# Two block rows of the causal attention turned by VectorE and a copy through DRAM, not by TensorE

## The chip, the cores and the metric

One core of one Trainium2 chip runs the whole program. The metric is device time in microseconds from launch to the end, taken as the median of three runs. A profiled execution gives the trace that the sections below read; its span runs from the first to the last instruction on the core.

## The reference

Two layers of attention follow each other. The first is a sliding window with four sink positions; the second is a mixture of four causal attentions, of which each position takes the two that its gate ranks highest.

```python
# layer 1: q, k, v are (4, 8, 768, 64); n_sink = 4, window = 128
scores = q @ k.T / 8
keep   = (pos_k < 4) | ((0 <= pos_q - pos_k) & (pos_q - pos_k < 128))
x      = softmax(where(keep, scores, -1e9)) @ v        # heads side by side: (4, 768, 512)

# layer 2: 4 experts, head size 64
w = softmax over the two largest of x @ w_gate
for e in range(4):
    qe, ke, ve = x @ wq[e], x @ wk[e], x @ wv[e]
    a    = softmax(where(causal, qe @ ke.T / 8, -1e9))  # (768, 768), lower triangle
    out += w[e] * (a @ ve @ wo[e])
```

## The kernel before

A sequence of 768 positions is six blocks of 128. Work comes in units. A unit of the first layer, `(b, n, 0)`, is a batch entry and a pair of heads; a unit of the second, `(b, n, 1)`, is a batch entry and a pair of experts (n is 0 or 1), so there are 16 of the one and 8 of the other. All is in fp32, products of the second layer in three passes over high and low parts.

`wide_rows` does the second layer's attention. A block row i has i + 1 key blocks, so rows 4 and 5 have five and six. Each row goes through the same steps, for both experts e: TensorE makes the scores in PSUM tiles `b` (L825, in two parts for five or six blocks, by `SPLIT`); VectorE masks, scales and takes the minimum of the negated scores into an SBUF tile `p` (L981); ScalarE takes the exponential with its sum (L989); `factor` makes one over the sum times the gate weight; GpSimd multiplies the row by it, in place (L996, `norm`). The row now has queries on the partitions, but the product with the values needs keys there. So `transposed` turns it part by part: TensorE transposes each 128x128 block in two halves of 64 partitions against `ident` (L878), into two PSUM tiles, which ScalarE (L707) or VectorE (L709) copies to `pt`, and then TensorE multiplies `pt` with the values into a PSUM tile `acc` (L851, called AV below). `finisher` splits `acc` into the high and low parts of `y` for the last product, `store`.

The first layer's `band_rows` uses the same steps on a band of two blocks, and the same transposes. Its q and k come from DRAM; for batch entries 1 to 3 they are loaded with their 32x32 squares already in swapped places (L1145), and VectorE transposes inside the squares (L799, L803).

The order of all instructions is made by `Plan` when the program is built: steps have a priority, costs and dependencies, and `emit` picks step after step for the five engines. `NUDGE` adds a number to the priority of single steps; `HURRY`, `STAY` and `BULK` weigh waiting, changes between kinds of matmul, and bulk. Where its plan has TensorE waiting, it puts matmuls on zeros (`fill`, L525). Buffers are rings (`kinds`: nine `p`, three `pt`, two `acc`). Each engine then runs its list strictly in order, and so does SyncE (SP), which issues every DMA.

TensorE runs four kinds of matmul, by how the array is split: transposes, scores and sink products (two row halves), AV (two column halves), and whole-array products (projections, values, `store`, called full below).

Of the kernel before, what the change touches and what calls it, by code (L numbers as in the profile page):

```python
# [37 lines left out]
    "busy_PE": 5.2, " ": -68.2, " busy_PE": 82.2, " busy_PE 0": 78.2, "sink_values_DVE": 13.5, " sink_values_DVE": -16.5,  # L38
    "load_SP": -45.6, " load_SP": 39.9, "again_SP": 20.9, " again_SP": 56.7, "sink_values_ACT": -27.6,
    " sink_values_ACT": 7.3, "sink_values_POOL": 52.1, " sink_values_POOL": 35.8, "sink_values_SP": -45.0,  # L40
    " sink_values_SP": -24.6, "weight_ACT": -52.5, " weight_ACT": 53.4, "weight_POOL": -34.8, " weight_POOL": 46.3,
    "000 ": -73.5, "000 load_SP": -144.1, "tr_PE": -1.9, "000 tr_PE": -132.5, "000 tr_PE 0": -105.3, "fn_DVEACT": -11.6,
    "000 fn_DVEACT": 132.8, "000 tr_PE 1": -54.6, "go_POOL": 0.7, "000 go_POOL": -36.7, "000 tr_PE 2": -47.6,
    "000 tr_PE 3": -19.2, "spread_POOL": -14.3, "000 spread_POOL": -25.7, "differences_POOL": 6.4,
    "000 differences_POOL": 24.4, "band_scores_PE": 0.5, "000 band_scores_PE": -115.3, "000 band_scores_PE 0": 8.1,
    "low_DVE": -53.0, "000 low_DVE": -79.5, "exp_ACT": 45.8, "000 exp_ACT": 63.9, "go_DVE": -42.9, "000 go_DVE": -204.0,
    "norm_POOL": -27.0, "000 norm_POOL": -84.7, "000 tr_PE 4": 23.5, "av_PE": -0.2, "000 av_PE": -0.9, "000 av_PE 0": -50.3,
    "000 band_scores_PE 1": -19.2, "000 tr_PE 5": -41.0, "000 av_PE 1": -26.4, "000 band_scores_PE 2": -53.5,
    "pick_DVE": -45.8, "000 pick_DVE": -22.7, "000 band_scores_PE 3": -19.7, "keep_POOL": -10.3, "000 keep_POOL": 6.5,
    "000 tr_PE 6": 35.3, "tri_DVE": -62.4, "000 tri_DVE": 59.9, "of_sinks_PE": -0.3, "000 of_sinks_PE": -1.5,  # L50
# [241 lines left out]
}  # L292

HURRY = 30.10
STAY = 41.79
BULK = -8.35
FILL_COST, FILL_KEEP, FILL_END = 220.0, 0.0, 130000.0
# [177 lines left out]
def kernel(  # L475
# [71 lines left out]
    def pool_cost(n):  # L547
        return 150 + 1.68 * n
# [18 lines left out]
    if banded:  # L567
# [28 lines left out]
        for t in (*slots["psk"], *slots["vs"]):  # L596
            nc.vector.memset(t.bitcast(F32), 0.0)
# [759 lines left out]
```

## Time and profile before

| | us |
|---|---|
| median of three runs (394.5 to 394.53) | 394.53 |
| the profiled execution, its own time | 394.46 |
| its span | 392.8 |
| TensorE busy | 383.0 |
| VectorE busy | 309.9 |
| ScalarE busy | 271.5 |
| GpSimd busy | 260.7 |

The 1.7 us between the profiled time and its span lie outside the recorded instructions. Busy time is a share of the span; idle time of an engine off the longest chain costs nothing. The granted clock of TensorE is full (1.0, its upper level) throughout.

### The profile page before, as it was taken

The numbers are of one execution on the slowest core, as the hardware profiler recorded it, in microseconds if no ns is written. First come the engines' busy times: TensorE is split into PE (matmuls) and PEld (weight loads), VectorE is DVE, ScalarE is ACT, GpSimd is POOL, SyncE is SP. The second block draws the span as 40 slices with busy tenths as digits, with TensorE's granted clock in tenths as the row PEclk, the third lists the DMA queues.
The fourth block names the chain that finished last, engine by engine and source line by source line (L and its number), as shares of the span: only waits on it lengthen the run. The fifth ranks groups of instructions, "written<-read, shape, count | busy, mean of one in ns | idle before, by whom it ended". The sixth has DMA issues, their size and how long they took to land.

```text
span 392.8 us, 12874 instructions
## 1 busy us (share of the span) xinstructions
PE 383.0 (98%) x4508; PEld 325.0 (83%) x4508; DVE 309.9 (79%) x1425; ACT 271.5 (69%) x970; POOL 260.7 (66%) x461
## 2 busy tenths in 40 slices
PE   6999999999999999999999999999999999999995
PEld 6777777988878888988888888988888888987874
DVE  5899999687999969679889959678679806748943
ACT  2898996256999957568869958549678804716830
POOL 5569999237999982668959864479958730038840
PEclk9999999999999999999999999999999999999999
DMA  7979997331165151523506200223000000012003
GB/s 164 220 148 172 197 174 127 56 49 43 43 100 105 44 107 55 83 83 82 82 2 119 47 0 5 40 109 95 2 3 2 3 3 2 2 53 109 3 28 134
DMA packets 124032, 28.42 MB, mean 72 GB/s; under 512 B 120576, under 2 KB 120576, under 8 KB 123968
## 3 DMA queue, kind: packets, MB, share of 16 engines
q1 hardware_dynamic: 123968, 27.61, 33.4%
q8 instruction: 35, 0.57, 0.6%
q14 instruction: 29, 0.24, 0.2%
HBM read 21.05 MB, written 6.29 MB: 70 GB/s over the span
## 4 chain that ended last, share of the span: by engine, by line
PE 81%; DVE 10%; POOL 3%; issue 2%; ACT 2%; DMA 1%; POOLq 0%; DVEq 0%; ACTq 0%
PE acc L851 18%; PE b L1177 18%; PE b L825 13%; PE b L878 10%; PE b L1204 9%; PE b L1251 9%; PE b L820 3%; DVE b L1078 2%; DVE p L1081 1%; PE acc L855 1%; DVE p L981 1%; DMA qn<-in_q_dram 1%; POOL v L680 1%; POOL p L1059 1%; DVE pt L709 1%
## 5 line engine op out<-in xcount | busy, mean ns | idle before, releaser
L996 POOL TENSOR_TENSOR p<-p,st 128x128 f32<-128x128 f32 (+5 forms) x96 | 87.2, 934 | 1.3
L707 ACT ACTIVATE pt<-b 128x256 f32<-128x256 f32 (+3 forms) x175 | 63.3, 396 | 12.6 <-PE b L878 8.8
L989 ACT ACTIVATE p<-p,st 128x384 f32<-128x384 f32 (+5 forms) x96 | 63.6, 669 | 9.4 <-DVE st L981 9.0
L825 PE MATMUL b<-ks,qs 64*128 64x260 f32 (+4 forms) x672 | 69.6, 323 | 0.4 <-DVE st L1081 0.2
L825 PEld LDWEIGHTS b<-ks,qs 64*128 64x128 f32 x672 | 53.0, 187 | 4.8 <-ACT pt L707 0.8
L878 PE MATMUL b<-ident,p 64*128 64x64 f32 x1120 | 55.2, 228 | 0.2 <-POOL p L1059 0.2
L878 PEld LDWEIGHTS b<-ident,p 64*128 64x128 f32 x1120 | 44.3, 138 | 11.8 <-issue 6.0
L1085 ACT ACTIVATE p<-p,st 128x132 f32<-128x132 f32 x128 | 51.1, 407 | 3.9 <-DVE st L1081 3.6
L981 DVE CUSTOM_DVE_ANT_0 p<-b,cmask 128x384 f32<-128x384 f32 (+3 forms) x96 | 45.3, 506 | 1.4 <-ACT o L707 1.1
L851 PE MATMUL acc<-pt,v 128*64 128x128 f32 x672 | 45.5, 278 | 0.6 <-DVE pt L709 0.5
L851 PEld LDWEIGHTS acc<-pt,v 128*64 128x64 f32 x672 | 36.2, 137 | 7.1 <-issue 3.9
L851 PE MATMUL acc<-pt,vn 128*64 128x128 f32 x448 | 41.5, 283 | 0.3 <-ACT p L989 0.3
L709 DVE COPY pt<-b 128x256 f32<-128x256 f32 (+3 forms) x81 | 34.6, 446 | 8.3 <-PE b L878 7.9
L1059 POOL TENSOR_TENSOR p<-p,st 128x520 f32<-128x520 f32 (+1 forms) x32 | 26.4, 834 | 14.8 <-DVE st L867 11.3
L1204 PE MATMUL b<-wvh,x 128*128 128x260 f32 x192 | 35.9, 285 | 0.0
L1177 PE MATMUL b<-x,wqh 128*128 128x256 f32 (+1 forms) x128 | 33.2, 345 | 0.1
L1104 POOL TENSOR_TENSOR p<-p,st 128x512 f32<-128x512 f32 x32 | 33.1, 1040 | 0.0
L1177 PE MATMUL b<-x,wkh 128*128 128x512 f32 (+1 forms) x128 | 32.8, 341 | 0.0
L1251 PE MATMUL b<-woh,y 128*128 128x512 f32 x96 | 32.8, 402 | 0.0
L1081 DVE CUSTOM_DVE_ANT_0 p<-b,pair_mask 128x132 f32<-128x132 f32 x128 | 32.6, 289 | 0.0
L1078 DVE COPY_PREDICATED b<-earlier,b 128x128 f32<-128x128 int32 x128 | 31.4, 288 | 1.2 <-PE b L820 1.1
L1052 ACT ACTIVATE p<-p,st 128x260 f32<-128x260 f32 (+1 forms) x64 | 29.0, 459 | 3.5 <-DVE st L1047 3.4
(132 smaller groups left out, 916.4 us busy)
## 6 DMA issues: line engine op xcount, KB each, us to landing
vn<-in_v_dram SPq DMA_DIRECT2D x32, 192.0 KB, 3.1
out_dram<-o SPq DMA_DIRECT2D x24, 256.0 KB, 2.0
qn<-in_q_dram SPq DMA_DIRECT2D x52, 96.0 KB, 2.4
kn<-in_k_dram SPq DMA_DIRECT2D x52, 96.0 KB, 2.4
qn<-in_q_dram SPq DMA_DIRECT2D x6, 192.0 KB, 4.1
kn<-in_k_dram SPq DMA_DIRECT2D x6, 192.0 KB, 4.4
o<-in_moe_wo_dram SPq DMA_DIRECT2D x2, 256.0 KB, 3.4
v<-in_moe_wk_dram SPq DMA_DIRECT2D x4, 128.0 KB, 3.8
```

Source lines behind the costliest of these rows:

```text
L707: nc.scalar.activation(dst(), src(), AF.Copy)
L825: nc.tensor.matmul(o, self.qs.t[hs, a, qs], self.ks.t[hs, b, ks], start=n == 0, stop=n == 2)
L851: nc.tensor.matmul(o[e * 64:e * 64 + 64], lhs, rhs, start=e not in self.begun, stop=last and self.done == len(self.steps))
L878: nc.tensor.transpose(t[g].t[:, n, :], x[gs], ident[gs, gs])
L981: nc.vector.tensor_tensor_reduce(out=one(e)[:, cs], in0=s2[e].t[:, :(c1 - c0) * 128], in1=mask(c0, c1), scale=times, scalar=st.t[:, 3, es] ...
L989: nc.scalar.activation(x, x, AF.Exp, bias=st.t[:, 0, es], scale=-1.0, accum_out=st.t[:, 1, es])
L996: nc.gpsimd.tensor_mul(x, x, st.t[:, 2, e:e + 1].to_broadcast([128, n * 128]))
L1078: nc.vector.copy_predicated(s2[e].t[:, :128], earlier.bitcast(I32), s2[e].t[:, SW:RW])
L1085: nc.scalar.activation(p.t[:, n, :], p.t[:, n, :], AF.Exp, bias=st.t[:, 0, n:n + 1], scale=-1.0, accum_out=st.t[:, 1, n:n + 1])
L1177: nc.tensor.matmul(t.t, w[a][:, c, es], X[b, c].t[:, x, cs], start=c == 0 and m == 0, stop=c == NCH - 1 and m == 2)
L1204: nc.tensor.matmul(t.t[:, :VW], X[b, c].t[:, a, qs], W["wv"][w][:, c, :], start=c == 0 and n == 0, stop=c == NCH - 1 and n == 2)
L1251: nc.tensor.matmul(t.t, Y[b, c].t[:, a, qs], W["wo"][w][:, c, :], start=c == 0 and n == 0, stop=c == EP - 1 and n == 2)
```

## The change

In five of the eight units of the second layer, rows 4 and 5 (five and six blocks) no longer go through `transposed`. A new function, `by_way_of_dram`, makes `norm` write the row into a second `p` tile with its 32x32 squares regrouped, lets VectorE transpose inside the squares, writes that tile to DRAM (`there`) with one DMA, and reads it back with four, one per 32 partitions, so that the squares change places. AV then takes its moving operand straight from that tile. In these units the two row groups are also done in reverse, rows 4 and 5 first. The set-up of the constant `lanes` moves ahead of the masks, that of `gsel`, `psk` and `vs` behind them. Nearly all of the 1200 entries of `NUDGE`, and three weights, have other numbers.

```diff
-HURRY = 30.10
-STAY = 41.79
-BULK = -8.35
+HURRY = 29.29
+STAY = 30.56
+BULK = -8.87
...
-        free = {PE: 2000.0, DVE: 3700.0, ACT: 2000.0, POOL: 6000.0, SP: 650.0}
+        free = {PE: 2000.0, DVE: 4500.0, ACT: 4000.0, POOL: 5300.0, SP: 650.0}
...
+    def by_way_of_dram(prio, acc, i, one, ps, cols, r, st, value):
 
-        for i in range(NB):
+        n, got, us = len(cols), [], []
+        for e in range(2):
+            u, there = buf("p", n * 128), buf("there", n * 128)
+            us.append(u)
+
+            def norm(u=u, e=e):
+                nc.gpsimd.tensor_mul(u.t.rearrange("p (b j c) -> p j b c", b=4, c=32), one(e).rearrange("p (j b c) -> p j b c", b=4, c=32),
+                                     st.t[:, 2, e:e + 1, None, None].to_broadcast([128, n, 4, 32]))
+
+            def back(u=u, there=there):
+                for b in range(4):
+                    nc.sync.dma_start(u.t[32 * b:32 * b + 32].rearrange("r (a x) -> r a x", a=4),
+                                      there.t.rearrange("(a r) (b x) -> b r a x", a=4, b=4)[b])
+            s = plan.step(prio - WIDE_N, {POOL: pool_cost(128 * n)}, norm, [r], [u], [ps[e], st])
+            s = plan.step(prio - WIDE_N, {DVE: 83 + 1.04 * 128 * n}, lambda u=u: nc.vector.transpose(u.t, u.t), [s], (), [u])
+            s = plan.step(prio - WIDE_N, {SP: 475}, lambda u=u, there=there: nc.sync.dma_start(there.t, u.t), [s], [there], [u], moves=MOVE * n)
+            got.append(plan.step(prio - WIDE_N - 10, {SP: 1900}, back, [s], (), [there, u], moves=MOVE * n))
+
+        def av():
+            acc.done += 1
+            for c, j in enumerate(cols):
+                for e in range(2):
+                    acc.add(i, e, value[0](j, e), us[e].t.rearrange("p (a j c) -> p j a c", a=4, c=32)[:, c], c == n - 1)
+        new, used = acc.bufs()
+        acc.steps.append(plan.step(prio + AV_LAG + 10, {PE: 218 * n}, av, got + value[1](cols), new, us + value[2] + used, fifo="av", mode="cols"))
+
+    def wide_rows(prio_of, pair, blocks, masks, value, weights, finish, groups, times=-scale, away=()):
+
+        for place, i in enumerate([i for lo, hi in (groups[::-1] if away else groups) for i in range(lo, hi)]):
...
             r = factor(prio - WIDE_N, st, sums, weights and (lambda i=i: weights[0](i)), weights and weights[1][i])
+            if i in away:
+                by_way_of_dram(prio, acc, i, one, ps, cols, r, st, value)
+                if i == hi - 1:
+                    finish(prio, acc)
+                continue
...
+    AWAY, MOVE = {u: (4, 5) for u in ((0, 0), (0, 1), (1, 0), (1, 1), (2, 0))}, 300
```

The first place is on TensorE, in the unit `(0, 0, 1)`. Before, the five-block row (tiles `p_91` and `p_92`, one for each expert) is turned by 20 transposes, of which the last six stand here; scores of the first layer and an AV on a turned part follow.

```order
L878 MATMUL b_120<-ident,p_92 128x64
L878 MATMUL b_123<-ident,p_92 128x64
L878 MATMUL b_120<-ident,p_91 128x64
L878 MATMUL b_123<-ident,p_91 128x64
L878 MATMUL b_120<-ident,p_92 128x64
L878 MATMUL b_123<-ident,p_92 128x64
L820 MATMUL b_121<-kx_82,qn_64 128x260
L820 MATMUL b_122<-kx_82,qn_64 128x260
L851 MATMUL acc_125<-pt_98,v_0_83 64x128 x4
```

After, no transpose of that row is left. Its tiles (now `p_91` and `p_93`) go into AV as they came back from DRAM; `v_0_85` holds the values.

```order
L817 MATMUL b_128<-kx_83,qn_65 128x128
L817 MATMUL b_127<-kx_83,qn_65 128x128
L848 MATMUL acc_132<-p_91,v_0_85 64x128
L848 MATMUL acc_132<-p_93,v_0_85 64x128
L848 MATMUL acc_132<-p_91,v_0_85 64x128
L848 MATMUL acc_132<-p_93,v_0_85 64x128
L848 MATMUL acc_132<-p_91,v_0_85 64x128
L848 MATMUL acc_132<-p_93,v_0_85 64x128
```

The row's transposes are gone, and AV comes in one piece for all five blocks. Over the whole program the transposes of `p` fall from 1120 to 900, and AV products stay at 688 rows. Runs of rows of one kind now change more often: counted over the whole list, changes into or out of AV (to or from scores, sinks or transposes; `fill` counts as AV, which splits the array in the same way) go from 175 to 182, and those into or out of full from 40 to 50; changes between scores and transposes go from 93 to 99.

The second place is SyncE's list, in that same unit. Before, it holds loads of the first layer alone (a `v` tile in two DMAs, a `q` or `k` tile in four).

```order
L1141 DMA vn_68<-in_v_dram 128x6x64 x2
L1145 DMA kn_66<-in_k_dram 32x24x32 x4
L1145 DMA qn_65<-in_q_dram 32x24x32 x4
L1145 DMA kn_67<-in_k_dram 32x24x32 x4
L1141 DMA vn_69<-in_v_dram 128x6x64 x2
L1141 DMA vn_70<-in_v_dram 128x6x64 x2
```

After, the writes to DRAM (`there`) and the reads back stand among those loads.

```order
L1171 DMA vn_71<-in_v_dram 128x6x64 x2
L959 DMA there_99<-p_91 128x640
L959 DMA there_100<-p_93 128x640
L955 DMA p_91<-there_99 32x4x160 x4
L955 DMA p_93<-there_100 32x4x160 x4
L959 DMA there_101<-p_88 128x768
L959 DMA there_102<-p_90 128x768
L1175 DMA kn_69<-in_k_dram 32x24x32 x4
L955 DMA p_88<-there_101 32x4x192 x4
L955 DMA p_90<-there_102 32x4x192 x4
L1171 DMA vn_72<-in_v_dram 128x6x64 x2
```

Each read waits for its write to land, each write for VectorE's transpose, and loads behind them in the list wait as well. SyncE's list has 100 DMAs more, 20 writes and 80 reads.

The third place is VectorE's list at the program's start. Before, the reduction to `gsel` stands ahead of the clearing of `psk` and `vs` and of the mask `cmask`.

```order
L585 MEMSET own 128x128
L590 MEMSET lanes 48x12
L595 TENSOR_REDUCE gsel<-lanes 48x4
L597 MEMSET psk_100 128x128
L597 MEMSET psk_101 128x128
L597 MEMSET psk_102 128x128
L597 MEMSET psk_103 128x128
L597 MEMSET vs_106 128x256
L597 MEMSET vs_107 128x256
```

After, it stands behind the masks and `cmask`; the clearing of `psk`, `vs` and of the staging tile `v_0_85` follows it, and then the first copy of the turned keys.

```order
L611 MEMSET tril 128x16
L616 MEMSET below 128x1 x4
L619 TENSOR_REDUCE gsel<-lanes 48x4
L621 MEMSET psk_106 128x128
L621 MEMSET psk_107 128x128
L621 MEMSET psk_108 128x128
L621 MEMSET psk_109 128x128
L621 MEMSET vs_112 128x256
L621 MEMSET vs_113 128x256
L673 MEMSET v_0_85 80x1024
```

GpSimd's two selections on `lanes` moved from behind its seven masks to ahead of them.

## Rows read from the trace of the kernel before

**Rows 1.** The page: span, busy time by engine, chain that ended last.

```profile
span 392.8 us, 12874 instructions
...
PE 383.0 (98%) x4508; PEld 325.0 (83%) x4508; DVE 309.9 (79%) x1425; ACT 271.5 (69%) x970; POOL 260.7 (66%) x461
...
PE 81%; DVE 10%; POOL 3%; issue 2%; ACT 2%; DMA 1%; POOLq 0%; DVEq 0%; ACTq 0%
```

**Rows 2.** Busy time in stretches of the span (us, instructions in brackets).

```profile
core 0: us, PE busy (x) PEld busy (x) DVE busy (x) ACT busy (x) POOL busy (x), PEclk, DMA share, GB/s
0.00:30.00 30.00, 26.20 (x298) 20.43 (x298) 23.58 (x149) 21.13 (x89) 18.63 (x46) 1.00 0.83 177
30.00:60.00 30.00, 29.42 (x385) 23.48 (x382) 29.00 (x145) 27.37 (x119) 29.06 (x55) 1.00 1.01 181
...
100.00:140.00 40.00, 39.69 (x572) 33.80 (x573) 38.56 (x197) 39.46 (x152) 38.04 (x63) 1.00 0.43 78
140.00:176.00 36.00, 36.00 (x365) 31.32 (x363) 26.31 (x117) 21.07 (x75) 21.08 (x39) 1.00 0.35 81
176.00:212.00 36.00, 35.60 (x480) 30.89 (x477) 32.42 (x151) 29.45 (x106) 28.68 (x45) 1.00 0.31 57
```

**Rows 3.** Timeline of TensorE from 200.97 us: start, duration, line, tiles, count.

```profile
200.97 0.44 PE L851 MATMUL acc<-pt,vn 128*64 128x128 f32 x4
201.34 0.59 PE L878 MATMUL b<-ident,p 64*128 64x64 f32 x12
201.74 0.87 PE L825 MATMUL b<-ks,qs 64*128 64x260 f32 x6
202.53 0.88 PE L851 MATMUL acc<-pt,v 128*64 128x128 f32 x12
203.34 0.46 PE L878 MATMUL b<-ident,p 64*128 64x64 f32 x8
203.61 1.33 PE L825 MATMUL b<-ks,qs 64*128 64x260 f32 x18
```

**Rows 4.** VectorE's groups by shape: count, busy us, mean ns, idle before.

```profile
L709 DVE COPY pt<-b 128x384 f32<-128x384 f32 x25 | 13.3, 548 | 6.2 <-PE b L878 6.2
L709 DVE COPY pt<-b 128x256 f32<-128x256 f32 x32 | 13.2, 414 | 0.7 <-PE b L878 0.6
...
L981 DVE CUSTOM_DVE_ANT_0 p<-b,cmask,st 128x384 f32<-128x384 f32 x16 | 9.3, 612 | 0.0
L803 DVE STREAM_TRANSPOSE kn<-kn 128x384 f32<-128x384 f32 x16 | 8.5, 558 | 0.2
```

**Rows 5.** GpSimd's groups by shape: `norm` of six and five blocks.

```profile
L996 POOL TENSOR_TENSOR p<-p,st 128x768 f32<-128x768 f32 x16 | 23.1, 1466 | 0.4
...
L996 POOL TENSOR_TENSOR p<-p,st 128x640 f32<-128x640 f32 x16 | 19.7, 1256 | 0.3
```

**Rows 6.** ScalarE's groups by shape: the exponential of six blocks.

```profile
L989 ACT ACTIVATE p<-p,st 128x768 f32<-128x768 f32 x16 | 15.0, 944 | 0.0
```

**Rows 7.** DMA issues on the page: count, KB each, us from issue to landing.

```profile
out_dram<-o SPq DMA_DIRECT2D x24, 256.0 KB, 2.0
qn<-in_q_dram SPq DMA_DIRECT2D x52, 96.0 KB, 2.4
```

**Rows 8.** Timeline of SyncE's queue at 28 us: start, duration, count.

```profile
28.35 2.30 SPq L1145 DMA_DIRECT2D qn<-in_q_dram  x4
```

**Rows 9.** TensorE's groups by shape: the products of `store`.

```profile
L1251 PE MATMUL b<-woh,y 128*128 128x512 f32 x96 | 32.8, 402 | 0.0
```

**Rows 10.** Timeline of the first 9 us, VectorE and TensorE.

```profile
4.64 0.16 DVE L595 TENSOR_REDUCE gsel<-lanes 48x4 f32<-48x12 f32 x1 [2.19 <-POOL lanes L592]
...
6.76 0.91 DVE L676 MEMSET v<- 80x1024 f32 x1 [0.16 <-issue]
...
7.80 0.34 DVE L709 COPY kx<-b 128x192 f32<-128x192 f32 x1
...
8.46 1.15 PE L820 MATMUL b<-kx,qn 64*128 64x260 f32 x8 [1.90 <-POOL kx L772]
```

More of the change, by code (lines that the diff above doesn't have):

```diff
@@ L37 @@
 NUDGE = {
[L38 to L47, printed above, removed]
@@ L48 @@
-    "000 band_scores_PE 1": -19.2, "000 tr_PE 5": -41.0, "000 av_PE 1": -26.4, "000 band_scores_PE 2": -53.5,
-    "pick_DVE": -45.8, "000 pick_DVE": -22.7, "000 band_scores_PE 3": -19.7, "keep_POOL": -10.3, "000 keep_POOL": 6.5,
-    "000 tr_PE 6": 35.3, "tri_DVE": -62.4, "000 tri_DVE": 59.9, "of_sinks_PE": -0.3, "000 of_sinks_PE": -1.5,
[48 rows of a table removed]
-    "most_DVE": -101.9, "001 most_DVE": -7.2, "rank_POOL": -188.0, "001 rank_POOL": 11.5, "values_ACT": 71.2,
-    "001 values_ACT": -6.2, "weigh_DVE": 72.0, "001 weigh_DVE": 28.4, "proj_PE": 4.8, "001 proj_PE": -19.9,
[40 rows of a table removed]
@@ L141 @@
-    "low_POOL": -7.3, "210 low_POOL": -76.1, "210 go_POOL": 14.6, "210 spread_POOL": 61.5, "210 differences_POOL": -9.1,
[150 rows of a table removed]
-}
-HURRY = 30.10
-STAY = 41.79
-BULK = -8.35
+    "busy_PE": -35.2, " ": -14.5, " busy_PE": 44.4, " busy_PE 0": 14.4, "sink_values_DVE": -63.9, " sink_values_DVE": -42.7,
+    "load_SP": -98.1, " load_SP": 27.8, "again_SP": -32.8, " again_SP": 2.5, "sink_values_ACT": -92.2,
+    " sink_values_ACT": 34.2, "sink_values_POOL": -20.4, " sink_values_POOL": 18.3, "sink_values_SP": -68.0,
@@ new lines @@
+    " sink_values_SP": -27.3, "weight_ACT": 41.3, " weight_ACT": -64.4, "weight_POOL": -75.8, " weight_POOL": -39.4,
+    "000 ": -57.8, "000 load_SP": 33.9, "tr_PE": -4.1, "000 tr_PE": -49.4, "000 tr_PE 0": -108.1, "fn_DVEACT": 23.4,
+    "000 fn_DVEACT": 18.5, "000 tr_PE 1": -6.2, "go_POOL": -57.8, "000 go_POOL": 133.7, "000 tr_PE 2": 7.5,
+    "000 tr_PE 3": 20.4, "spread_POOL": -50.7, "000 spread_POOL": -8.4, "differences_POOL": 173.3,
+    "000 differences_POOL": -37.7, "band_scores_PE": 1.1, "000 band_scores_PE": -64.2, "000 band_scores_PE 0": -75.3,
@@ new lines @@
+    "low_DVE": -52.3, "000 low_DVE": 30.9, "exp_ACT": 274.5, "000 exp_ACT": 57.1, "go_DVE": -15.0, "000 go_DVE": 58.1,
+    "norm_POOL": -83.7, "000 norm_POOL": 4.7, "000 tr_PE 4": -9.3, "av_PE": 1.6, "000 av_PE": -20.4, "000 av_PE 0": -24.7,
+    "000 band_scores_PE 1": 14.2, "000 tr_PE 5": 30.2, "000 av_PE 1": -25.8, "000 band_scores_PE 2": 16.4,
+    "pick_DVE": -15.0, "000 pick_DVE": 56.0, "000 band_scores_PE 3": 21.0, "keep_POOL": -105.0, "000 keep_POOL": 9.3,
+    "000 tr_PE 6": -6.3, "tri_DVE": -17.0, "000 tri_DVE": -17.4, "of_sinks_PE": -0.7, "000 of_sinks_PE": -10.2,
[26 rows of a table added]
@@ new lines @@
+    "110 load_SP": -51.3, "turn_DVE": 119.5, "110 turn_DVE": -77.7, "110 go_POOL": 93.6, "110 spread_POOL": 30.9,
[20 rows of a table added]
+    "most_DVE": -123.6, "001 most_DVE": -1.2, "rank_POOL": 48.2, "001 rank_POOL": 26.8, "values_ACT": -124.6,
+    "001 values_ACT": -18.0, "weigh_DVE": -107.5, "001 weigh_DVE": -60.0, "proj_PE": -8.3, "001 proj_PE": -16.4,
[5 rows of a table added]
+    "001 factor_POOL": 87.0, "001 norm_POOL": -120.4, "by_way_of_dram_DVE": -34.9, "001 by_way_of_dram_DVE": -73.8,
+    "by_way_of_dram_SP": -39.1, "001 by_way_of_dram_SP": 69.0, "back_SP": -58.9, "001 back_SP": -1.1, "001 av_PE": 13.4,
[30 rows of a table added]
@@ L297 @@
+    "turn_ACT": -12.9, "210 turn_ACT": 14.9, "low_POOL": 90.7, "210 low_POOL": 8.9, "210 go_POOL": -18.8,
[150 rows of a table added]
+}
+HURRY = 29.29
+STAY = 30.56
+BULK = -8.87
 FILL_COST, FILL_KEEP, FILL_END = 220.0, 0.0, 130000.0
@@ L512 @@
              "x": (6, 2 * S, F32R), "kx": (2, NB * SW, F32), "v2": (1, 1536, F32), "y0": (1, 2 * S, F32R), "y1": (1, 2 * S, F32R), "p": (9, 768, F32),
-             "dv": (2, 512, F32), "pt": (3, 1024, F32), "psk": (4, 128, F32), "sk": (2, 128, F32R), "vs": (2, 4 * D, F32R),
+             "dv": (2, 512, F32), "there": (4, 768, F32), "pt": (3, 1024, F32), "psk": (4, 128, F32), "sk": (2, 128, F32R), "vs": (2, 4 * D, F32R),
              "o": (2, 512, F32), "gate": (2, 4 * NB * E, F32), "gates": (1, 2 * NB * E * E, F32), "st": (6, 20, F32),
@@ L529 @@
     banks = ctx.enter_context(tc.tile_pool(name="banks", bufs=1, space=bass.MemoryType.PSUM))
+    dram = ctx.enter_context(tc.tile_pool(name="dram", bufs=1, space=bass.MemoryType.DRAM))
     ctx.enter_context(tc.manual_schedule())
-    slots = {tag: [(banks if tag in PSUM else consts).tile([128, w], dt, name=f"{tag}_{x}") for x in range(n)]
+    slots = {tag: [(banks if tag in PSUM else dram if tag == "there" else consts).tile([128, w], dt, name=f"{tag}_{x}") for x in range(n)]
              for tag, (n, w, dt) in kinds.items()}
@@ L567 @@
     if banded:
+        lanes = consts.tile([48, 3, 4], F32, name="lanes")
+        nc.vector.memset(lanes, 1.0)
+        for sign, base in ((1, 0), (-1, 3)):
+            nc.gpsimd.affine_select(out=lanes, in_=lanes, pattern=[[-16 * sign, 3], [-4 * sign, 4]], compare_op=OP.is_ge, fill=0.0,
+                                    base=base, channel_multiplier=sign)
         for i, ns in ((0, n_sink), (1, n_sink)):
@@ L587 @@
                                 base=0, channel_multiplier=-1)
-        lanes = consts.tile([48, 3, 4], F32, name="lanes")
-        nc.vector.memset(lanes, 1.0)
-        for sign, base in ((1, 0), (-1, 3)):
-            nc.gpsimd.affine_select(out=lanes, in_=lanes, pattern=[[-16 * sign, 3], [-4 * sign, 4]], compare_op=OP.is_ge, fill=0.0,
-                                    base=base, channel_multiplier=sign)
-        gsel = consts.tile([48, 4], F32, name="gsel")
-        nc.vector.tensor_reduce(gsel, lanes.rearrange("p t n -> p n t"), axis=AX.X, op=OP.add)
-        for t in (*slots["psk"], *slots["vs"]):
-            nc.vector.memset(t.bitcast(F32), 0.0)
     else:
@@ L624 @@
         nc.vector.memset(below[:, e:e + 1], e - 1.5)
+    if banded:
+        gsel = consts.tile([48, 4], F32, name="gsel")
+        nc.vector.tensor_reduce(gsel, lanes.rearrange("p t n -> p n t"), axis=AX.X, op=OP.add)
+        for t in (*slots["psk"], *slots["vs"]):
+            nc.vector.memset(t.bitcast(F32), 0.0)
     W, W_READY = {}, {}
@@ L943, in transposed_band @@
                                    [pt] + value[2] + diff[2] + used, fifo="av", mode="cols"))
-    def wide_rows(prio_of, pair, blocks, masks, value, weights, finish, groups, times=-scale):
-        for i in range(NB):
+    def by_way_of_dram(prio, acc, i, one, ps, cols, r, st, value):
[23 more added lines that the diff above has]
+        for place, i in enumerate([i for lo, hi in (groups[::-1] if away else groups) for i in range(lo, hi)]):
             lo, hi = next(g for g in groups if g[0] <= i < g[1])
@@ L950, in wide_rows @@
                 acc = Acc(lo, hi)
-            prio = prio_of(i)
+            prio = prio_of(place)
             cols, mask = blocks[i], masks[i]
@@ L1188, in second @@
                   (lambda i: WT[b].t[:, 2, i, 2 * ep:2 * ep + 2], WT_READY[b]),
-                  finisher((b, ep), f"y{ep}", Y, Y_READY), groups)
+                  finisher((b, ep), f"y{ep}", Y, Y_READY), groups, away=AWAY.get((b, ep), ()))
     def values(b, groups, prio_of):
```

469 rows, old and new, of the table NUDGE are left out of this document.

## The prediction

> **What bounds the kernel now.** I read the page first. TensorE is busy for 383.0 of a span of 392.8 us, and the chain of work that ended last lies on it for 81% [rows 1]. The reader is to see that waiting is scarce: what takes time off TensorE's list can come back as time, and what only relieves another engine can not. Second came the table by stretches [rows 2]. TensorE is full from 100 us on (39.69 of 40, 35.60 of 36, 47.82 of 48); only up to 60 us does it miss some (26.20 and 29.42 of 30). But it is not alone there: from 30 to 60 us VectorE is busy for 29.00 of 30 and GpSimd for 29.06, from 100 to 140 us VectorE for 38.56 of 40, ScalarE for 39.46, GpSimd for 38.04. So there are stretches in which four engines are full at once, and others (176 to 212, 212 to 260) where VectorE has a tenth to a fifth to spare. Third, the timeline of TensorE gives what one instruction takes of its list, from start to start [rows 3]; the mean durations overlap and would count it several times.
>
> **What is removed on TensorE.** In five units, rows of 5 and 6 blocks, two experts: 22 blocks a unit, each turned by two instructions, so 5 x 44 = 220, which is also what the order shows (1120 to 900). Twelve transposes take 0.40 us until the next kind starts (201.34 to 201.74), eight take 0.27 (203.34 to 203.61): four more for 0.13, so 0.0325 us each [rows 3]. 220 x 0.0325 = **7.2 us off the list**.
>
> The Trainium skill, in VectorE: DVE Perf Modes, sections The three transpose paths and Rules for kernel authors, speaks against the change: for a full 128x128 block it recommends TensorE, at 390 ns for a bf16 block, since VectorE turns only 32x32 squares. By that figure 110 blocks would be an estimated 43 us of TensorE; the timeline has 0.065 us for an fp32 block, as transposes run closely behind each other, and it decides the sum. Its advice counts the operation alone, not which engine is full.
>
> **What is added on TensorE.** AV products are as many as before. The kinds of work change more often: by the order, 7 more changes into or out of AV, 10 more into or out of full products, 6 more between scores and transposes. An AV instruction takes 0.055 us (twelve for 0.81 us, four for 0.37, so 0.44 for eight); four are 0.22, and the change to transposes is the remaining 0.15 [rows 3]. Between transposes and scores there is next to nothing (12 x 0.0325 = 0.39 of 0.40). For full products I take the same 0.15, an estimate; bounds are 0 and 0.3 for each. 17 x 0.15 = **2.6 us back on the list** (1.1 to 4.1). Net: 4.6 us off, between 3.1 and 6.1.
>
> AV now reads its moving operand in runs of 32 out of the regrouped tile, which no row shows. Bounds: 0.055 us as now, or twice that for 110 products of two instructions, 12.1 us. I take nothing, since count and width are those of the AV row; the other end is a rival.
>
> **The start.** VectorE's reduction to `gsel` waits 2.19 us for GpSimd; the clearing of the staging tile ends at 7.67 us, the first copy of keys starts at 7.80, and TensorE's first scores, which need it, at 8.46 after a wait of 1.90 [rows 10]. After, the selections come first on GpSimd and the reduction late on VectorE, so the wait goes, and the first scores can come up to 2 us earlier. What is late next are the loads: the DMA engines are 0.83 busy up to 30 us and full (1.01) from 30 to 60 [rows 2]. Bounds 0 and 2 us; I take **1.0 us**.
>
> **What is added elsewhere.** VectorE gets 20 transposes, ten of 640 and ten of 768 columns. The row has 558 ns for 384. From below, with the slope of the copies (548 less 414 for 128 columns, 1.05 ns a column): 826 and 960 ns, 17.9 us in all. From above, in proportion: 930 and 1116, 20.5 us. I take 19.2. It loses copies to `pt`: by the order twelve of 384 columns and six of 256, 12 x 0.548 + 6 x 0.414 = 9.1 us [rows 4]. Net 10.1 us more, 320 of about 387: hidden as long as the added work falls where VectorE has room.
>
> GpSimd makes as many `norm` instructions, 1.47 and 1.26 us each [rows 5]. Their regrouped output stands in no row; the nearest is the same product with plain output. Bounds: no change, or double, 27 us more on an engine that is busy for 260.7 [rows 1]. I take no change.
>
> SyncE issues 100 more DMAs, about 0.58 us each (2.30 for four) [rows 8]. A write of 320 or 384 KB should land like a 256 KB output, 2.0 us, or up to 3.0 in proportion; a read of 80 or 96 KB like a load of 96 KB, 2.4 us [rows 7]. The engines have room from 100 us on, where their share is 0.23 to 0.43 [rows 2].
>
> The way of a six-block row, from its last scores to AV, nothing queued: two minima of 0.61 [rows 4], one exponential 0.94 [rows 6], two `norm` 2.9 [rows 5], one transpose 1.0, a write 0.6 + 2.5, eight reads' issue 4.6 and landing 2.4; some 16 us. What covers it is what stands on TensorE's list in between. The tightest of the ten rows is the five-block one of unit (1, 0, 1), whose way is some 15 us: between its last scores and its AV stand 56 transposes (1.8 us), 30 AV products (3.3), 59 score products (6.3, at 0.107: six for 0.79 less the change [rows 3]), 8 sink products (0.8, priced as scores) and 24 of `store` (at most 8.2, at 0.34, busy time by count [rows 9]), about 20 us. The others have 22 to 50. So the round trip is hidden if queues on GpSimd, VectorE and SyncE cost a row less than about 5 us at the tightest and 6 elsewhere. If that cover goes, TensorE stands at AV, and all behind it in its list waits, as do the `p` and `acc` tiles.
>
> **The sum.** The profiled execution took 394.46 us (the median is 394.53, so no correction): 394.46 - 4.6 - 1.0 = 388.9, say **389.0 us**.
>
> **The rivals.** *VectorE keeps the gain.* The 10.1 us fall where VectorE is already full, as from 100 to 140 us. If half is passed on, 388.9 + 5.1 = 394.0, no change; if all, 399.0. For it: 38.56 of 40. Against it: the plan can move work, and 36 us from 176 on hold 3.6 us of room, 48 from 212 on hold ten [rows 2].
>
> *The round trip comes late (slower).* One mechanism: SyncE works in order, a read stands behind the wait for its write, which stands behind VectorE's transpose, and loads and outputs stand behind both; TensorE then waits at the head of its list at an AV of a returned row. Each of ten rows pays; from 0.56 us a row on (5.6 / 10) the change loses. With 1.5 us a row it is 388.9 + 15 = 403.9; with 1.0 it is 398.9. For it: 15 to 16 us of way against 20 of cover at the tightest, and GpSimd full for 38.04 of 40 where units overlap [rows 2]. Against it: nine rows with 22 to 50 us.
> The Trainium skill, in DMA: Bandwidth & Descriptors, section on the anatomy of one DMA, has about 2.0 us fixed for each DMA (for GpSimd's path), mostly the receipt of the write, heaviest for DRAM; by it the two legs would be an estimated 4 us and more in series, which agrees with the 2.0 and 2.4 us of the rows.
>
> *AV reads the regrouped tile slowly (slower).* Twice 0.055: 388.9 + 12.1 = 401.0. From 0.025 us an instruction on the gain is gone.
>
> *More comes back.* The start gives its whole 2 us and the changes of kind cost their lower bound: 394.46 - 6.1 - 2.0 = 386.4.
>
> **How the numbers follow.** Forecast (387 to 391.5): 0.55. VectorE keeps half or more (393 to 399): 0.18. Round trip late: 0.14, most of it between 394 and 400. AV slow: 0.04. More comes back (386 to 387): 0.09. The range 386.0 to 397.0 leaves out about 2 in 10. Beyond 0.2% (0.8 us, about what this measurement can tell): faster is the forecast, the last rival, and 0.07 of the VectorE case, 0.71; within it 0.07; slower 0.22.
>
> **What would show it.** Right: TensorE's busy time down by 4 to 5 us, with waits at AV of `p` near zero; 20 VectorE transposes of 0.8 to 1.1 us; first scores near 6.5 us. Wrong: idle time of TensorE in front of AV of `p` that ends on a DMA (round trip), waits of TensorE for VectorE from 100 us on (VectorE), or returned AV instructions more than 0.055 us apart (slow reading).

## The result and the profile after

The changed kernel takes **391.27 us** (median of four runs, 390.92 to 391.6) against 394.53 for the kernel before, measured beside it: a ratio of 0.9911, 95% interval 0.9892 to 0.9931. It is faster by 3.3 us; the forecast was 5.5 (389.0), and its range of 386 to 397 holds the time, which lies at the upper end of the forecast's own part (387 to 391.5). The profiled execution took 391.6 us with a span of 389.9.

The page of the changed kernel, the same three lines as in [rows 1]:

```profile
span 389.9 us, 12672 instructions
...
PE 381.2 (98%) x4276; PEld 318.4 (82%) x4276; DVE 318.2 (82%) x1422; ACT 263.4 (68%) x953; POOL 261.5 (67%) x461
...
PE 86%; ACT 7%; DVE 4%; issue 1%; POOL 0%; DVEq 0%; ACTq 0%
```

TensorE loses only 1.8 us of busy time, where the prediction named 4 to 5 us as the sign of being right. VectorE has 8.3 us more and ScalarE 8.1 less, since copies to `pt` are gone from both and VectorE's transposes are new. The chain lies on TensorE for 86% in place of 81%.

The stretches of [rows 2]:

```profile
0.00:30.00 30.00, 28.34 (x303) 22.07 (x303) 25.06 (x160) 23.14 (x101) 20.55 (x49) 1.00 0.85 178
30.00:60.00 30.00, 29.28 (x361) 23.66 (x362) 28.35 (x131) 22.95 (x100) 28.72 (x57) 1.00 0.96 177
100.00:140.00 40.00, 39.79 (x490) 32.62 (x484) 37.96 (x173) 32.64 (x124) 31.15 (x54) 1.00 0.69 154
140.00:176.00 36.00, 35.67 (x375) 30.54 (x375) 31.91 (x151) 24.93 (x91) 25.85 (x44) 1.00 0.46 107
176.00:212.00 36.00, 35.32 (x442) 29.93 (x440) 30.64 (x145) 29.23 (x105) 27.74 (x49) 1.00 0.64 144
```

From 0 to 30 us TensorE has 2.1 us more work done than before (26.20). From 100 to 140 us ScalarE falls from 39.46 to 32.64 and GpSimd from 38.04 to 31.15, so in this stretch four engines are no longer full. GpSimd's work has moved, not shrunk: over the whole span it is 261.5 us, and was 260.7. From 140 to 212 us TensorE now misses 1.0 us of 72, where it missed 0.4.

The groups by shape on VectorE, GpSimd and TensorE, which answer to [rows 4, 5]:

```profile
L958 DVE STREAM_TRANSPOSE p<-p 128x768 f32<-128x768 f32 x10 | 9.6, 959 | 0.7 <-POOL p L950 0.7
L958 DVE STREAM_TRANSPOSE p<-p 128x640 f32<-128x640 f32 x10 | 8.3, 828 | 0.0
...
L950 POOL TENSOR_TENSOR p<-p,st 128x768 f32<-128x768 f32 x10 | 14.7, 1469 | 0.1
L950 POOL TENSOR_TENSOR p<-p,st 128x640 f32<-128x640 f32 x10 | 12.6, 1256 | 1.6 <-POOL vs L1042 0.8 <-ACT pt L704 0.5 <-PE b L875 0.2
...
L848 PE MATMUL acc<-pt,v 128*64 128x128 f32 x452 | 31.9, 279 | 0.1
L848 PE MATMUL acc<-p,v 128*64 128x128 f32 x220 | 14.1, 276 | 0.0
```

VectorE's transposes cost 17.9 us, GpSimd's regrouped `norm` costs what the plain one cost (1466 and 1256 ns), and AV from the regrouped tile is no slower than from `pt` (0.055 us an instruction from start to start in both).

The DMA issues of the way through DRAM on the page (count, KB each, us from issue to landing), beside [rows 7]:

```profile
there<-p SPq DMA_DIRECT2D x10, 384.0 KB, 3.2
p<-there SPq DMA_DIRECT2D x40, 96.0 KB, 2.4
there<-p SPq DMA_DIRECT2D x10, 320.0 KB, 2.3
p<-there SPq DMA_DIRECT2D x40, 80.0 KB, 2.8
```

The waits of TensorE, longest sums first (us in total, times, longest); none on the whole list is for `p<-there`:

```profile
PE b L1292 <- DVE lanes L566: 1.1, 1, 1.1
PE acc L852 <- ACT sk L704: 1.0, 2, 0.8
PE acc L852 <- POOL vs L1042: 0.5, 1, 0.5
PE b L822 <- ACT pt L704: 0.5, 1, 0.5
```

The start, which answers to [rows 10]:

```profile
3.09 0.15 DVE L619 TENSOR_REDUCE gsel<-lanes 48x4 f32<-48x12 f32 x1
...
4.51 0.91 DVE L673 MEMSET v<- 80x1024 f32 x1 [0.16 <-issue]
...
6.62 0.36 DVE L706 COPY kx<-b 128x192 f32<-128x192 f32 x1 [1.20 <-PE b L875]
...
7.14 0.49 PE L817 MATMUL b<-kx,qn 64*128 64x128 f32 x4
```

The wait of 2.19 us for `gsel` is gone, and the first scores come 1.3 us earlier, at 7.14.

**Where TensorE's time went.** For each TensorE instruction I took the time to the start of the next. Inside a run of one kind the median per shape is its price in the list; the first instruction of another kind gives the price of the change (the median for each pair of kinds, over both traces); what is over is waiting.

| us, profiled executions | before | after | difference |
|---|---|---|---|
| list of work | 338.7 | 331.1 | -7.6 |
| changes of kind | 32.1 | 35.3 | +3.2 |
| waiting beyond these | 9.3 | 10.35 | +1.0 |
| zero products at the start | 3.8 | 4.6 | +0.75 |
| before the first and after the last | 8.9 | 8.6 | -0.25 |
| span | 392.8 | 389.9 | -2.9 |

Of the 7.6, the transposes are 6.9 and zero products of `fill` 0.7. Of the waiting, the first 40 us give back 0.7 and the stretch from 200 to 220 us takes 2.3. The zero products are the same twenty before and after; their length differs between kernels of one and the same start (3.77 to 4.37 among those below), so I ascribe it to nothing. Where a change of kind ends and a wait begins hangs on the price that is taken for a change: with the mean of a pair of instructions as the price in the list, the same traces give 3.9 us more for changes and 0.2 more for waiting. The sum of the two, some 4.2 us, stays.

### The profile page after: what moved, and what is told of

Its sections match the earlier page's. It is cut to its first block, busy times and chain, and to the rows that moved or that the text cites. A ratio compares the mean times of both kernels' runs of the same rounds, so it can differ in the third digit from the quotient of the medians.

```text
span 389.9 us, 12672 instructions
## 1 busy us (share of the span) xinstructions
PE 381.2 (98%) x4276; PEld 318.4 (82%) x4276; DVE 318.2 (82%) x1422; ACT 263.4 (68%) x953; POOL 261.5 (67%) x461
## 4 chain that ended last, share of the span: by engine, by line
PE 86%; ACT 7%; DVE 4%; issue 1%; POOL 0%; DVEq 0%; ACTq 0%
PE acc L848 20%; PE b L1207 18%; PE b L822 12%; PE b L875 9%; PE b L1234 9%; PE b L1281 9%; PE b L817 5%; ACT p L1014 2%; PE acc L852 2%; DVE p L1006 2%; ACT pt L704 1%; ACT p L1115 1%; PE b L1292 1%; PE b L521 1%; DVE p L1111 1%
## 5 line engine op out<-in xcount | busy, mean ns | idle before, releaser
L1014 ACT ACTIVATE p<-p,st 128x128 f32<-128x128 f32 (+5 forms) x96 | 63.6, 668 | 13.6 <-DVE st L1006 13.1
L704 ACT ACTIVATE pt<-b 128x256 f32<-128x256 f32 (+3 forms) x156 | 55.1, 380 | 13.0 <-PE b L875 12.5
L1026 POOL TENSOR_TENSOR p<-p,st 128x128 f32<-128x128 f32 (+5 forms) x76 | 60.8, 823 | 1.3
L875 PE MATMUL b<-ident,p 64*128 64x64 f32 x900 | 47.7, 228 | 0.0
L1089 POOL TENSOR_TENSOR p<-p,st 128x256 f32<-128x256 f32 (+1 forms) x32 | 26.4, 834 | 26.8 <-DVE st L864 7.9
L1207 PE MATMUL b<-x,wqh 128*128 128x512 f32 (+1 forms) x128 | 33.3, 345 | 0.0
L1207 PE MATMUL b<-x,wkh 128*128 128x512 f32 (+1 forms) x128 | 32.7, 342 | 0.0
L848 PE MATMUL acc<-pt,v 128*64 128x128 f32 x452 | 31.9, 279 | 0.1
L1082 ACT ACTIVATE p<-p,st 128x128 f32<-128x128 f32 (+1 forms) x64 | 28.7, 452 | 4.6 <-DVE st L1077 4.3
L848 PEld LDWEIGHTS acc<-pt,vn 128*64 128x64 f32 x448 | 24.7, 136 | 7.8 <-issue 2.0
L1234 PEld LDWEIGHTS b<-wvh,x 128*128 128x128 f32 x192 | 30.0, 188 | 1.0 <-DVE st L1077 0.3
```

The lines of the kernel that those rows point to most:

```text
L704: nc.scalar.activation(dst(), src(), AF.Copy)
L848: nc.tensor.matmul(o[e * 64:e * 64 + 64], lhs, rhs, start=e not in self.begun, stop=last and self.done == len(self.steps))
L875: nc.tensor.transpose(t[g].t[:, n, :], x[gs], ident[gs, gs])
L1014: nc.scalar.activation(x, x, AF.Exp, bias=st.t[:, 0, es], scale=-1.0, accum_out=st.t[:, 1, es])
L1026: nc.gpsimd.tensor_mul(x, x, st.t[:, 2, e:e + 1].to_broadcast([128, n * 128]))
L1207: nc.tensor.matmul(t.t, w[a][:, c, es], X[b, c].t[:, x, cs], start=c == 0 and m == 0, stop=c == NCH - 1 and m == 2)
```

## The experiments

The first theory, from the prediction: TensorE's list is the bound, what leaves it comes back less the dearer changes of kind, and the way through DRAM is hidden with some us to spare. Its rivals: VectorE's new transposes, or the way through DRAM, keep part of the gain. The runs of before beside these had medians of 394.43 to 394.74.

**The way through DRAM left out.** The lines of `by_way_of_dram`, with the writes and reads empty:

```diff
-                for b in range(4):
+                for b in range(0):
...
-            s = plan.step(..., lambda u=u, there=there: nc.sync.dma_start(there.t, u.t), [s], [there], [u], moves=MOVE * n)
+            s = plan.step(..., lambda: None, [s], [there], [u], moves=MOVE * n)
```

> The changed kernel with the 20 writes to DRAM and the 80 reads left out: the squares stay in their wrong places, and TensorE takes the tiles straight from VectorE; all other lists are the same. Theory (the trip is hidden): 391.3 within 0.6. Rival (round trip): the missing gain comes back, 388.5 to 390 us.

Measured: 392.39 us, ratio 0.9935 (0.9919 to 0.9951). Leaving out 100 DMAs gives nothing back; the time is even 1.1 us above that of the change, for a reason that stays open. So no part of the missing gain is a wait for the way through DRAM.

**VectorE's transposes left out.**

```diff
-            s = plan.step(..., lambda u=u: nc.vector.transpose(u.t, u.t), [s], (), [u])
+            s = plan.step(..., lambda: None, [s], (), [u])
```

> The changed kernel with VectorE's 20 transposes inside the squares left out (17.9 us of VectorE in the profile), so that the tiles travel unturned. Theory (TensorE's list is the bound): at most 1 us less than 391.3, and that in the stretch from 200 to 216 us, where TensorE lost 1.6 us. Rival (VectorE keeps the gain): 2 to 5 us less, 386 to 389.

Measured: 391.17 us, ratio 0.9907 (0.9889 to 0.9924). VectorE's busy time falls to 304.1 us and the time stays. VectorE does not keep the gain either.

**The set-up in its old places**, the rest as changed:

```diff
-        lanes = consts.tile([48, 3, 4], F32, name="lanes")
...
+        lanes = consts.tile([48, 3, 4], F32, name="lanes")
...
+        gsel = consts.tile([48, 4], F32, name="gsel")
...
-        gsel = consts.tile([48, 4], F32, name="gsel")
```

> The changed kernel with the set-up of lanes, gsel, psk and vs in its old places; the plan and all else are the same. Theory (the start forecast at 1.0 us gave almost nothing, since the first turned loads and later waits up to 40 us set the pace): within 0.6 of 391.3. Rival (it gave its 1 to 2 us, and the loss is elsewhere): 392.3 to 393.3.

Measured: 392.6 us, ratio 0.9958 (0.9942 to 0.9973). The start is worth 1.3 us. By the table above that leaves about 2 us of gain for all the rest, though 7.6 us left the list, or 4.4 net of the changes of kind.

**Work put back on TensorE.** Products by zeros into the accumulators of the returned rows, one for each of 45 blocks:

```diff
             for c, j in enumerate(cols):
+                if c:
+                    o = acc.b.t[:, (i - acc.lo) * 128:(i - acc.lo) * 128 + 128]
+                    nc.tensor.matmul(o[:64], nought[:, :64], nought, start=False, stop=False)
```

> The changed kernel with 45 products of zeros added between the products of the returned tiles (two instructions of 0.055 us each, 4.95 us on TensorE's list, adding zero to the sums). Theory (the list is the bound, almost without slack): 4.4 to 5.2 us more, 395.7 to 396.5. Rival (another engine or the round trip is what TensorE runs up against, so that its list has slack there): 0 to 3 us more.

Measured: 400.29 us, ratio 1.0137 (1.0116 to 1.0158): 9.0 us more than the change, twice the price that I had expected for 45 products. The same with a zero product for each column half, 90 in all (`for e in range(2 if c else 0)` around the product into `o[64 * e:64 * e + 64]`):

> The change with 90 products by zeros, one for each column half, ahead of 45 of the 55 pairs of AV products of the returned rows. If two products for the two halves run at once, a pair costs 0.109 us and 45 cost 4.9: 391.3 + 4.9 = 396.2 (395.3 to 396.7, if some falls into waits). If each product had its own price of 0.109, as the 9.0 us for 45 unpaired ones could also be read with other costs around them, 9.8: 401. If TensorE had room: below 394.

Measured: 400.77 us, ratio 1.0143 (1.0122 to 1.0164): 9.5 us more. My price missed a second time, because a product is two instructions. TensorE's timeline in this run:

```profile
108.20 0.44 PE L848 MATMUL acc<-p,v 128*64 128x128 f32 x4
108.47 0.39 PE L967 MATMUL acc<-nought 128*64 128x128 f32 x4
108.69 0.39 PE L848 MATMUL acc<-p,v 128*64 128x128 f32 x4
108.91 0.39 PE L967 MATMUL acc<-nought 128*64 128x128 f32 x4
```

A pair of products, four instructions, takes 0.22 us from start to start; 45 pairs are 9.9 us, of which 9.5 come out as time. Ninety products cost hardly more than 45 (9.5 and 9.0 us): the second one of a pair runs beside the first. The Trainium skill, TensorEngine Tiling (Array Packing), section Key Properties, says that different tiles of the array can load and multiply in parallel; the two times agree. So what is added to TensorE's list at these places of the changed kernel comes out as time nearly whole. The question is whether what is taken off comes back in the same way.

**Transposes taken off the kernel before.** Before's own order, only the first block of each part (two instructions) is turned in rows 4 and 5 of five units, so 180 of 220 transposes are left out:

```diff
-            for m in range(n):
+            for m in range(1 if few else n):
```

> The kernel before, in its own order, with 180 of the 220 transposes left out (each step of those rows keeps its first two; the copies and products go on with stale data). Theory (0.0325 us each, and the list is the bound): 5.85 us less than before, so 388.4 to 389.4, were TensorE not to run up against the copies. Rival (from 100 to 140 us the other engines are as full as TensorE): 1 to 3.5 us less, 391 to 393.5.

Measured: 394.03 us, ratio 0.9988 (0.9974 to 1.0002), so 0.4 us for 180 x 0.0325 = 5.9 us of list. The first theory falls here. By the same account as above the list falls by 5.7 us in this run and the waiting rises from 9.3 to 14.5. TensorE's waits from 100 to 300 us, first in the kernel before:

```profile
PE acc L851 <- ACT p L989: 0.3, 1, 0.3
PE b L825 <- DVE st L1081: 0.2, 1, 0.2
PE b L825 <- DVE pt L922: 0.2, 1, 0.2
```

And in this run:

```profile
PE b L825 <- DVE st L1081: 0.9, 3, 0.3
PE b L825 <- ACT pt L707: 0.9, 2, 0.6
PE b L820 <- DVE st L1081: 0.3, 1, 0.3
```

TensorE now stands at scores that need a PSUM tile `b` which VectorE (masks and minima) or ScalarE (a copy to `pt`) has not yet cleared. These rows name 1.9 of the 5.2 us that the waiting rises by; the other gaps are too short to be listed, but by the account nearly all of the 5.2 us lies ahead of or between score products. Hence the second theory: TensorE and the engines that clear its PSUM were level in the kernel before, and the change gains because the copies to `pt` go away together with the transposes. The rival: something else in before's order is late, and copies do not matter.

**Transposes and their copies taken off the kernel before.** The same, and the 40 copies to `pt` in these rows cut to 64 columns:

```diff
-        moved = [evacuate(prio, lambda g=g: pt.t[:, :, 64 * g:64 * g + 64], lambda g=g: t[g].t[:, :n, :], 64 * n, ...
+        moved = [evacuate(prio, lambda g=g: pt.t[:, :1 if few else n, 64 * g:64 * g + 64], lambda g=g: t[g].t[:, :1 if few else n, :], 64 * n, ...
```

> The kernel before, in its own order, with 180 of the 220 transposes left out (as in the run that gave 394.0) and the 40 copies to pt behind them cut to the 64 columns of the one transpose that stays (the other columns of pt, and with them the output, are not computed); the way through DRAM is in neither. The change takes both away, the earlier run only the transposes. Theory A: what TensorE then waits for are VectorE and ScalarE, which clear its PSUM tiles, and the copies to pt are their share of it; with about 0.3 us less for each of 40 copies (12 us over two engines) the transposes' time comes back: 394.0 less 3 to 5, 389 to 391. Theory B: what is late is the chain of the softmaxes in before's order (masks, minima, exponentials, GpSimd), which the copies hardly touch: 393 to 394, at most 1 us under the earlier run.

Measured: 391.5 us against 394.74, ratio 0.9908 (0.989 to 0.9925): 3.2 us. TensorE's waits from 100 to 300 us in it:

```profile
PE b L825 <- DVE st L1081: 0.8, 3, 0.3
PE acc L851 <- ACT p L989: 0.3, 1, 0.3
PE b L825 <- ACT pt L707: 0.2, 1, 0.2
```

The waits for ScalarE's copy fall from 0.9 to 0.2; those for VectorE's masks stay. The time is 2.5 us under that of the run with the transposes alone, so theory B falls; it also misses the 389 to 391 of theory A by 0.5 us. And **the copies alone**, with all transposes in place:

> The kernel before with all its transposes, and only the 40 copies to pt cut to 64 columns (the other columns of pt, and with them the output, are not computed). If TensorE's list alone is the bound, as the prediction had it: 394.5, no change. Theory A (TensorE and the engines that clear its PSUM are balanced, and each gives little alone): 393 to 394.2. If the copies are the bound by themselves: below 392.

Measured: 393.31 us against 394.74, ratio 0.9965 (0.9951 to 0.9979): 1.4 us. So transposes alone give 0.4, copies alone 1.4, both together 3.2, more than the sum of the two. For before's order the second theory stands: neither side was the bound by itself. Even so only 3.2 of the 5.9 us come back. That the change, in its other order, gains in the same way is not shown. The mirror image, work added to the kernel before or taken off the changed one, was not run either, so added and removed work are compared in two different orders.

**The slack of the way through DRAM.** The last of the four reads of each tile is issued again:

```diff
+                nc.sync.dma_start(u.t[96:128].rearrange("r (a x) -> r a x", a=4),
+                                  there.t.rearrange("(a r) (b x) -> b r a x", a=4, b=4)[3])
```

> The changed kernel, but the last of the four reads of every returned tile is issued a second time, behind the first. Theory (TensorE's list is the bound and the round trip is hidden): 391.3 us as the changed kernel, within 0.6, with no wait of TensorE at the products of returned tiles, though each of the ten rows comes back some 3 us later (0.58 of issue and 2.4 of landing). Rival (the missing 2.3 us of the forecast gain are waits for the round trip): each of ten rows pays a part of those 3 us, so 394 to 401 us.

Measured: 423.99 us, ratio 1.0741 (1.0714 to 1.0768), 32.7 us more than the change. The waits of TensorE and of SyncE's queue that are new in it:

```profile
PE acc L848 <- DMA p<-there: 22.1, 8, 4.1
...
SPq L957 <- DMA p<-there: 39.0, 20, 3.1
```

The delay is larger than I had meant: the second read overwrites the first, so SyncE stands until that has landed, 39.0 us over 20 tiles, and what is queued behind it stands too. Some 4.5 us a row (39.0 and 20 issues of 0.30, over ten rows) were too much, and the time lies far above the 394 to 401 us of the rival. A gentler delay, two more writes of each tile to DRAM that nobody reads:

```diff
+            def out(u=u, there=there):
+                nc.sync.dma_start(there.t, u.t)
+                for _ in range(2):
+                    spares.append(spares.pop(0))
+                    nc.sync.dma_start(spares[0][:, :n * 128], u.t)
```

> The change with each of the 20 writes issued three times, twice more to DRAM tiles that nobody reads. By the 0.344 us of a write's issue SyncE reaches the reads 0.7 us later for each tile, and since the reads overwrite the tile that the extra writes take, they also stand behind the landing of these: some 0.7 to 1.5 us a tile, up to 3 us a row, against the 4.5 us a row by which the run with a read issued again held SyncE up (it waited 39.0 us in all for the first reading to land, and cost 32 us). If the way had the 4 to 5 us to spare that the prediction gave the tightest row, no change: 391 to 392. If it has next to none, so that SyncE's delay comes out at TensorE row by row: 20 tiles with 0.7 to 1.5 us, 400 to 415 or so. If about half of the rows have a few us to spare: 393 to 398.

Measured: 418.78 us, ratio 1.0589 (1.0562 to 1.0616), 27.5 us more than the change and above the worst case that was expected (415). TensorE's wait in it:

```profile
PE acc L850 <- DMA p<-there: 15.0, 8, 3.2
```

Two stretches with such waits (columns as in [rows 2], the granted clock third from the end):

```profile
80.00:120.00 40.00, 35.05 (x360) 27.43 (x358) 32.57 (x150) 25.04 (x89) 27.10 (x47) 0.91 0.77 205
120.00:160.00 40.00, 34.55 (x408) 28.79 (x410) 30.43 (x124) 28.03 (x99) 27.02 (x44) 0.94 0.78 202
```

TensorE's busy time in this run is 391.0 us for the same 4276 instructions (381.2 in the change), and the granted clock falls below 1.00 where it waits. Waits at returned tiles (15.0), one for ScalarE (3.2) and the 9.8 us of longer work make 28.0 of the 28.9 us that the span is longer. The run does more than hold SyncE up: its extra writes load the DMA engines too (a share of 0.77 from 80 to 120 us, 0.65 in the change), and the way's own DMAs land later, in the order of the rows below after 4.1, 2.5, 3.1 and 3.6 us, where the change has 3.2, 2.4, 2.3 and 2.8:

```profile
there<-p SPq DMA_DIRECT2D x10, 384.0 KB, 4.1
p<-there SPq DMA_DIRECT2D x40, 96.0 KB, 2.5
there<-p SPq DMA_DIRECT2D x10, 320.0 KB, 3.1
p<-there SPq DMA_DIRECT2D x40, 80.0 KB, 3.6
```

How much of the 27.5 us is SyncE's delay and how much the later landing was not separated.

That the way has little slack can be seen in the trace of the change itself. For the five-block row of unit (1, 0, 1), the last two reads on SyncE and the AV that needs them:

```profile
L955 SPq DMA_DIRECT2D p<-there x2: 430/433/436, 179.7 to 180.2; - x2
...
DMA to landing us min/median/max: 4.4/4.5/4.7
```

```profile
184.68 0.55 PE L848 MATMUL acc<-p,v 128*64 128x128 f32 x6
```

The last read is issued at 180.2 and lands 4.4 to 4.7 us later, at 184.6 to 184.9; AV starts at 184.68. For this row nothing is left. Read in the same way, seven of the ten rows have 3.2 us or less between the last landing and AV, the other three 4.3 and more.

**The plan without its numbers.** Two kernels with the changed code and weights and all entries of `NUDGE` at zero, one with `AWAY` empty (no row goes through DRAM), one with the five units:

```diff
-            s.prio += sum(NUDGE.get(name, 0.0) for name in s.part)
+            s.prio += sum(0.0 * NUDGE.get(name, 0.0) for name in s.part)
...
-    AWAY, MOVE = {u: (4, 5) for u in ((0, 0), (0, 1), (1, 0), (1, 1), (2, 0))}, 300
+    AWAY, MOVE = {}, 300
```

> The changed kernel with all entries of NUDGE taken as zero and no unit going through DRAM (AWAY empty), so an order by the plan's own rules with all rows turned by TensorE. It is the base for the next run. Both theories: slower than both kernels, by an unknown amount (400 to 425 us).

> The same with all entries of NUDGE as zero, and the five units through DRAM as in the change. Theory (the way through DRAM takes 7.2 us off TensorE's list, and the changes of kind give some back, whatever the order): 2 to 8 us under the run without it. Rival (the gain is that of the new numbers in the order, the way itself brings nothing): within 2 us of it, or slower.

Measured: 404.96 us (ratio 1.0257, 1.0238 to 1.0276) without the way through DRAM, 420.14 (1.0641, 1.0619 to 1.0664) with it. TensorE's longest wait in the second:

```profile
PE b L875 <- POOL p L1026: 9.3, 8, 4.3
```

With the plan's own priorities the way through DRAM, and the reversal of the two row groups that comes with it, make the kernel 15.2 us slower. TensorE has no listed wait for a returned tile; it waits for GpSimd, whose `norm` of other rows comes late. So the way through DRAM does not gain in every order. Before's numbers with the way through DRAM, and the new numbers without it, were not run, so structure and order are told apart only at numbers of zero.

## Why the prediction was right in sign and too high in size

- **The list.** Forecast 7.2 us off TensorE's list; 6.9 by the account above, and 0.7 of `fill` besides. As a sum of work this was right, and so was the net of list and changes of kind together (4.6 forecast, 4.4 by the account).
- **The step that failed** is the one before it: "waiting is scarce: what takes time off TensorE's list can come back as time". In before's order 5.9 us off the list gave 0.4 us, and 3.2 with the copies gone too; about half came back at best. In the change itself less is lost: by the account, behind the first 40 us waiting takes 1.7 us more than before, where the prediction put such waits at nothing. Work that is added does come out (9.5 of 9.9 us). In these runs a full TensorE tells what more work costs, and not what less of it gives. The prediction had the row for it, four engines full from 100 to 140 us [rows 2], and used it for two rivals, VectorE's added transposes and GpSimd's part of the round trip, but not against the gain itself. It also booked the missing copies to `pt` (9.1 us on VectorE, and ScalarE's, not booked at all) as room and not as part of the gain.
- **The changes of kind.** Forecast 2.6 us for 17 changes, measured 3.2 for all kinds of change together (3.9 with the other price), which is 0.19 each if it is laid on the 17 alone, inside the bounds. The Trainium skill, TensorEngine Tiling (Array Packing), section Key Properties, says that a change of the tiling mode drains TensorE; the changes that cost time here agree.
- **New waits.** Forecast none; from 200 to 220 us TensorE loses 2.3 us more than before, where VectorE is busy for 18.83 of 20 and ScalarE for 18.72. The longest is at 214.77, sink products that wait 0.81 us for ScalarE's `sk`. It is there with the same 0.8 us when the way through DRAM is left out, so it is not the way itself; whether it belongs to the new numbers or to the rows' reversal was not isolated.
- **The start.** Forecast 1.0 us, measured 1.3 by the run with the old set-up. The first scores come at 7.14, not near 6.5.
- **VectorE, GpSimd, AV.** The transposes cost the lower bound (828 and 959 ns), and without them the time is the same; `norm` and AV are unchanged, as forecast. Both rivals on them fall.
- **The way through DRAM.** Hidden, as forecast: no wait of TensorE for `p<-there`. The writes land in 2.3 and 3.2 us and the reads in 2.8 and 2.4, near the prices taken, and an issue takes 0.34 (write) and 0.43 us (read) at the median, less than 0.58. But the margin was wrong. Cover was counted as work on TensorE's list, 20 us at the tightest and 22 to 50 elsewhere, and the way as 15 to 16 us with nothing queued; in the trace the queues take the rest, the tightest row has nothing left and seven of ten have 3.2 us or less. The condition, that queues cost the tightest row less than about 5 us, was met by an order that spends these 5 us. The rival had the mechanism right, SyncE in order and TensorE at the head of its list; both delayed runs show TensorE waiting there (22.1 and 15.0 us). That the margin held was luck in part: the working gave a row 5 us to spare, and the tightest had none.
- **The sum.** Forecast 5.6 us for the profiled execution, 2.9 seen. The account has 0.6 more for changes, 1.0 more waiting where 1.0 less was forecast, and 0.75 more zero products at the start; against it stand 0.4 more off the list and 0.25 at the ends. How much of the gain the new numbers found, and how much the missing transposes and copies, stays open.

## What to carry to other kernels

A full engine can have two prices: here what was added cost nearly its whole time (9.5 of 9.9 us), while what was removed gave back only as far as the engines that clear its buffers could follow (0.4 of 5.9 us, and 3.2 with their copies gone too). So take the work off both sides of the buffer at once and check the pair, not the one. A transfer that hides completely may still have no slack; read the time between its landing and its first reader before loading that queue with anything more. Such a change and its order are one thing: under the plan's own priorities the same rows cost 15 us.

## What was not expected of the hardware

- Two products into the two column halves take the time of one: 45 unpaired ones added 9.0 us, 90 paired ones 9.5.
- A wait of TensorE can cost more than its length. In the run with three writes the granted clock is 0.91 and 0.94 in the stretches 80 to 120 and 120 to 160 us, where the change has 1.00: it falls below its upper level where TensorE has just waited 3.2 and 1.7, and 2.4 and 3.0 us (0.68 from 108 to 116 us, 0.66 from 153 to 160). The same instructions took 9.8 us longer; 15.0 us of waits at returned tiles went with 27.5 us of time. The run with a read issued again shows the same, 22.1 us of such waits and 7.7 us of longer work. That the waits bring the clock down is read from their places, not tested.
- The same wait does not always bring the clock down. In the profiled executions with the old set-up and with the copies alone, the granted clock was 0.72 from 6 to 12 us, behind waits of 1.7 and 1.5 us ahead of the first scores, and they took 1.1 and 1.4 us more than the medians of their kernels; the kernel before shows 1.00 there behind a wait of 1.9.
- VectorE's transpose inside 32x32 squares costs 558, 828 and 959 ns for 384, 640 and 768 fp32 columns, about 1.05 ns for each column more, and GpSimd's product writes a regrouped tile at the price of a plain one (1469 against 1466 ns).
